# Retention and two mixture-of-experts layers in one kernel: the planned scheme of passes 1 and 2 used for pass 0 as well

## The chip, the cores and the metric

One core of one Trainium2 chip runs the whole program. The metric is device time in microseconds (us) for one execution, as the median of several; one further execution was recorded by the hardware profiler, and all rows below come from that one. The engines are PE (matrix products; PEld is its weight load), DVE, ACT and POOL (elementwise work), and SP, whose queue issues nearly all DMAs. Each engine works through its own instruction list in order.

## The reference, cut to what is computed

```python
# q, k, v: (4, 8, 576, 64); x: N = 2304 tokens of D = 512; E = 8 experts, F = 1024
ret = scale * (q @ k.T) * Dmat;  x = ret @ v          # retention
e = argmax(x @ w_gate)                                # layer 1: one expert for each token
x[mask_e] = gate * (relu(x[mask_e] @ w1[e]) @ w2[e])
P = exp(x @ w_gate2 - max); 8 times: rows and columns of P normalised   # layer 2
out = sum over e of P[:, e] * (relu(x @ w1[e]) @ w2[e])  # every token, every expert
```

Layer 2 is the bulk: all 2304 tokens go through all 8 experts. Each fp32 product is made of three products of a high and a low part (hi*hi, hi*lo, lo*hi), so each weight and each activation is split: ACT makes hi (a cast), DVE or POOL makes lo (value minus hi).

## The kernel before

Layer 2 runs in three passes of 768 tokens (`NP = 3`, `GRP = 384` columns for each half). In a pass an expert has four *units* (`i` = 0 to 3), each a quarter of its first product `x @ w1`. That product is done by a Strassen-Winograd scheme: 7 block products in place of 8 (`product(j)`, j = 0 to 6), each of 6 matmuls of 128x384, so 42 matmuls a unit. It needs sums of blocks of x (made once a pass, `xsums`, `xsplit`, `load_pass` in the changed kernel) and of w1 (made in pass 0 and stored, already split, in DRAM as `w1s`).

**Pass 0** (lines 1085 to 1292) is written out by hand. `unit()` takes the weights from a ring of slots (`Slot`, `split_step`, `keep_up`, lines 150 to 285): a kind of prefetch, in which two raw 256-column loads make two slots of kind "sums" (L255, L256 on POOL, L263 on ACT, L219 on DVE). The second product, `second()` (L1100 to L1102), is the plain one: 36 matmuls of 128x512 a unit, and it is always that of the unit before, set between the block products of the present one. So a unit has 42 + 36 matmuls, an expert 312. Into the first units other work is put with `mids`: the last second product of layer 1 (`last_steps`, 96 matmuls of 128x280, in unit 0), and the second gate with its 8 rounds of normalising (`sinkhorn`, `gate_step`). Until P is there, expert 0's result is kept unweighted, and `weigh` (L1124 to L1128) multiplies it afterwards.

**Passes 1 and 2** (lines 1299 to 1742) are made by a planner. Every instruction is a `Task` with an engine, an estimated duration and what it comes after; a list scheduler plays the tasks through, in order of due time, and issues the instructions of each engine in the order that results. The order on PE, `line`, is fixed ahead: the first product of expert s, with pieces of the second product of expert s-1 in its gaps (`GAPS`). The second product has 7 block products here too: `chunk2` (L1566 to L1568), 42 chunks of 6 matmuls of 128x256, 252 an expert, beside 168 of the first product (L1385 to L1387). For it, sums and splits are made of the hidden values (L1502, L1505, L1512, L219 on `sl`) and of w2 (L1502 and L1505 on POOL, L1512, L219 on `wbl`). Results go through `evict` (L1583, L1585) to `ya`. w1 is not made anew: `wa` is loaded from `w1s` (L1367).

Between the two lies a change of memory: `early.close()` gives the whole memory of pass 0 back, and the planner's tiles take it. `out` is written by indirect DMAs from POOL (L104).

```python
        GAPS = (1, 1, 2, 2, 1, 3, 0.5)
        for s in range(first_s, last_s + 1):
            b = [g2[s - 1, j, kh, t] for j in range(7) for kh in range(2) for t in range(HB)] if s > first_s else []
            ...
                    for j in range(7):
                        line.append(g1[s, i, j])
                        owed += GAPS[j]
                        while owed >= 1:
                            ...
                                line.append(b.pop(0))
```

Of the kernel before, what the change touches and what calls it, by code (L numbers as in the profile page):

```python
# [28 lines left out]
RAW = 5  # L29
LO_DVE = 256  # L30
LO_AT = 256
HI_DVE = ()
# [3 lines left out]
def kernel(  # L36
# [16 lines left out]
    dbg=None,  # L53
# [15 lines left out]
    raw_p = ctx.enter_context(tc.tile_pool(name="raw", bufs=RAW))  # L69

    early = ExitStack()
    ring_p = early.enter_context(tc.tile_pool(name="ring", bufs=4))
    sum_p = ctx.enter_context(tc.tile_pool(name="sums", bufs=1, side="right"))
# [66 lines left out]
    WEIGH_ACT = (0, 2, 4)  # L140
# [4 lines left out]
    WAIT = 4  # L145
    BEHIND = 6
    SPOTS = "bd"
# [6 lines left out]
    class Slot:  # L154
        def __init__(self, kind, parts, col=0):
            self.kind, self.parts, self.col = kind, parts, col
            slots.append(self)
            for r in parts:
                raws[r][3] = len(slots)
# [12 lines left out]
    def w1_slots(i):  # L172
        for f in range(2):
            Slot("plain", [part((i, f, r), lambda i, f, r: rows2(expert(w11, i), r)[:, :, f * half:(f + 1) * half])
                           for r in range(2)])

    def w2_slots(i):
        for f in range(2):
            Slot("plain", [part((i, f, r), lambda i, f, r: rows2(expert(w12, i), 2 * f + r))
# [26 lines left out]
    def load_more():  # L206
        while n_load[0] < n_known[0]:
# [5 lines left out]
            t = raws[n][2] = raw_p.tile([128, 1024], F32, tag="raw", name="raw")  # L213
# [7 lines left out]
    def split_step(n=1, force=False):  # L221
        for _ in range(n):
# [7 lines left out]
            need = c.parts[s // 2] if c.kind == "plain" else max(c.parts)  # L230
# [3 lines left out]
            if s == 0:  # L234
                c.hi = ring_p.tile([128, 2048], F32R, tag="hi", name="hi")
                c.lo = ring_p.tile([128, 2048], F32R, tag="lo", name="lo")
            if c.kind == "plain":
                x = raws[c.parts[s // 2]][2]
                o, i = s * 512, s % 2 * 512
                if s in HI_DVE:  # L240
# [1589 lines left out]
```

## Time and profile before

| | us |
|---|---|
| median of 3 runs (1873.04 to 1876.92) | 1876.38 |
| the profiled execution: time / span of its instructions | 1880.59 / 1878.8 |
| retention and layer 1, up to the first product of layer 2 | 0 to 377.8 |
| pass 0 | 377.8 to 890.8 |
| passes 1 and 2, to the last matmul | 890.8 to 1868 |

A page row of an engine gives its busy time, the share of the span and the count. A row of a stretch gives, for each engine, busy time and instruction count (x), then the granted share of TensorE's clock, the mean busy share of the DMA engines and GB/s. Since matmuls are pipelined, the count of matmuls in a stretch tells more than PE's busy time.

### The profile page before, as it was taken

Reading aid. Unit: us, or ns where it says so; the run is one execution under the profiler, and the core shown is the slowest. Engines: PE = TensorE matmul, PEld = TensorE weight load, DVE = VectorE, ACT = ScalarE, POOL = GpSimd, SP = SyncE. Lnnn points to the kernel's source line nnn. Section 1 sums busy time; section 2 is a strip of 40 time slices with the busy share of each in tenths; the row PEclk is TensorE's granted clock in tenths of the full one; section 3 lists DMA queues with packets and bytes.
Section 4 is the critical chain, followed back from the end, with each engine's and each line's share of the span. In section 5 each row is a group of like instructions: output and inputs, shape, how many; then the busy total and the mean of one; then the engine's idle time right before and its main releaser. Section 6 shows DMA issues by size and latency. Waiting matters only on the chain.

```text
span 1878.8 us, 32676 instructions
## 1 busy us (share of the span) xinstructions
PE 1803.9 (96%) x12227; PEld 1720.0 (92%) x12227; DVE 1233.2 (66%) x2239; ACT 892.2 (47%) x1718; POOL 575.1 (31%) x599
## 2 busy tenths in 40 slices
PE   7778999999999999999699999999999999999997
PEld 6657999998899999998599999999999999999997
DVE  6864446556655554555267777877887777777777
ACT  2243455544434343433355555555656555555553
POOL 4544567632332333334211121111223121111211
PEclk9998999999999999999899999999999999999998
DMA  9955555565555555543755555655556545555430
GB/s 261 239 162 176 174 196 185 175 217 184 185 186 185 185 185 204 199 174 121 229 167 152 165 160 169 186 162 153 162 165 197 155 154 161 167 158 166 145 123 35
DMA packets 194577, 325.13 MB, mean 173 GB/s; under 512 B 24547, under 2 KB 97507, under 8 KB 194408
## 3 DMA queue, kind: packets, MB, share of 16 engines
q1 hardware_dynamic: 190264, 312.29, 52.2%
q0 software_dynamic: 3712, 9.96, 1.7%
q8 instruction: 99, 1.62, 0.4%
q10 hardware_dynamic: 432, 0.69, 0.1%
q14 instruction: 70, 0.57, 0.1%
HBM read 248.28 MB, written 74.61 MB: 172 GB/s over the span
## 4 chain that ended last, share of the span: by engine, by line
PE 84%; DVE 3%; ACT 1%; issue 1%; DMA 1%; POOL 0%; SPq 0%; ACTq 0%; DVEq 0%; POOLq 0%
PE b L1568 8%; PE b L1567 8%; PE b L1566 8%; PE b L1385 8%; PE b L1386 8%; PE b L1387 8%; PE b L1100 5%; PE b L1102 5%; PE b L1101 5%; PE b L1170 4%; PE b L1172 4%; PE b L1171 4%; PE b L669 3%; PE b L671 3%; PE b L670 3%
## 5 line engine op out<-in xcount | busy, mean ns | idle before, releaser
L1566 PE MATMUL b<-wbh,sh 128*128 128x256 f32 x1344 | 379.7, 282 | 2.1 <-DVE ya L1585 2.1
L1568 PE MATMUL b<-wbh,sl 128*128 128x256 f32 x1344 | 380.3, 283 | 0.5 <-DVE sl L219 0.4
L1567 PE MATMUL b<-wbl,sh 128*128 128x256 f32 x1344 | 380.6, 283 | 0.0
L1385 PE MATMUL b<-ch,wa 128*128 128x384 f32 x896 | 304.8, 340 | 17.6 <-ACT kp L1391 7.4
L1386 PE MATMUL b<-cl,wa 128*128 128x384 f32 x896 | 302.3, 337 | 0.0
L1387 PE MATMUL b<-ch,wa 128*128 128x384 f32 x896 | 300.8, 336 | 0.0
L219 DVE TENSOR_TENSOR sl<-hq,sh 128x768 fp32r<-128x768 f32 x224 | 223.7, 1004 | 85.3 <-ACT sh L1512 83.2
L1568 PEld LDWEIGHTS b<-wbh,sl 128*128 128x128 f32 x1344 | 257.5, 192 | 0.9 <-DVE sl L219 0.9
L1566 PEld LDWEIGHTS b<-wbh,sh 128*128 128x128 f32 x1344 | 255.6, 190 | 2.3 <-ACT sh L1512 2.3
L1567 PEld LDWEIGHTS b<-wbl,sh 128*128 128x128 f32 x1344 | 257.2, 191 | 0.0
L219 POOL TENSOR_TENSOR lo<-raw,hi 128x256 fp32r<-128x256 f32 x192 | 171.8, 905 | 266.1 <-ACT hi L243 263.7
L1512 ACT CAST sh<-hq 128x768 fp32r<-128x768 f32 x224 | 184.5, 832 | 72.0 <-PE b L1567 67.3
L219 DVE TENSOR_TENSOR lo<-raw,hi 128x256 fp32r<-128x256 f32 (+1 forms) x256 | 152.2, 598 | 89.0 <-ACT hi L243 78.6
L1400 ACT ACTIVATE hq<-hq 128x384 f32<-128x384 f32 x192 | 100.9, 525 | 230.4 <-DVE hq L1397 228.4
L1385 PEld LDWEIGHTS b<-ch,wa 128*128 128x128 f32 x896 | 170.6, 190 | 22.7 <-ACT kp L1391 7.8
L1585 DVE SCALAR_TENSOR_TENSOR ya<-b,P,ya 128x256 f32<-128x256 f32 x312 | 142.2, 478 | 66.3 <-PE b L1568 65.0
L1502 POOL TENSOR_TENSOR raw<-raw 128x512 f32<-128x512 f32 x63 | 88.7, 1409 | 313.9 <-DVE wbl L219 219.6
L1386 PEld LDWEIGHTS b<-cl,wa 128*128 128x128 f32 x896 | 171.3, 191 | 0.0
L1387 PEld LDWEIGHTS b<-ch,wa 128*128 128x128 f32 x896 | 168.9, 189 | 0.0
L1170 PE MATMUL b<-ch,hi 128*128 128x384 f32 x448 | 151.6, 338 | 0.3
L1172 PE MATMUL b<-ch,lo 128*128 128x384 f32 x448 | 150.5, 336 | 0.0
L1171 PE MATMUL b<-cl,hi 128*128 128x384 f32 x448 | 150.3, 336 | 0.0
(212 smaller groups left out, 3729.8 us busy)
## 6 DMA issues: line engine op xcount, KB each, us to landing
wa<-w1s SPq DMA_DIRECT2D x192, 512.0 KB
raw<-in_moe_w_dram SPq DMA_DIRECT2D x128, 512.0 KB
w1s<-hi SPq DMA_DIRECT2D x32, 896.0 KB
w1s<-lo SPq DMA_DIRECT2D x32, 896.0 KB
raw<-in_moe_w_dram SPq DMA_DIRECT2D x108, 256.0 KB
wa<-w1s SPq DMA_DIRECT2D x64, 256.0 KB
sums<-in_moe_w_dram SPq DMA_DIRECT2D x20, 256.0 KB
kT<-in_kT_dram SPq DMA_DIRECT2D x18, 256.0 KB
```

The lines of the kernel that those rows point to most:

```text
L219: eng.tensor_tensor(lo, x, hi.bitcast(F32), ALU.subtract)
L1170: nc.tensor.matmul(ps, a, xh[:, r, :], start=first and r == 0, stop=False, skip_group_check=True)
L1171: nc.tensor.matmul(ps, a, xl[:, r, :], start=False, stop=False, skip_group_check=True)
L1172: nc.tensor.matmul(ps, b, xh[:, r, :], start=False, stop=r == 1, skip_group_check=True)
L1385: nc.tensor.matmul(ps, a, xh[:, r, :], start=first, stop=False, skip_group_check=True)
L1386: nc.tensor.matmul(ps, a, xl_[:, r, :], start=False, stop=False, skip_group_check=True)
L1387: nc.tensor.matmul(ps, b, xh[:, r, :], start=False, stop=r == 1, skip_group_check=True)
L1512: nc.scalar.copy(o.tile[0], src.tile)
L1566: nc.tensor.matmul(ps, hh[:, r, c], wh[:, r], start=st, stop=False, skip_group_check=True)
L1567: nc.tensor.matmul(ps, hh[:, r, c], wl[:, r], start=False, stop=False, skip_group_check=True)
L1568: nc.tensor.matmul(ps, hl[:, r, c], wh[:, r], start=False, stop=kh == 1 and r == 1, skip_group_check=True)
L1585: nc.vector.scalar_tensor_tensor(o, ps, sc_, o, ALU.mult, ALU.add)
```

## The change

- **Pass 0 joins the plan.** `unit`, `second`, `finish`, `weigh` and the slots for layer 2's weights are removed. The planner now runs over all 24 pairs of pass and expert (`n_exp = NP * E`).
- **w1 in pass 0** is made by tasks (`first_weights`): for each unit two loads of 128 columns (runs of 512 bytes; before, 256 columns for two units), four sums of 128x256 on POOL, a cast on ACT and a lo on DVE for each of four pieces (three of 512 columns, one of 256), and a store of each piece to `w1s`.
- **w2 in pass 0** and the second product go as in the later passes.
- **The last unit's second product of layer 1** is nine PE tasks (`tail`): four ahead of expert 0, the others between the first block products of its unit 0.
- **The second gate** is twelve PE tasks (`gate`), six between expert 0's products (`GATES`), six in expert 1's (`in_gap`); each is followed by a DVE task of 1.6 us that issues nothing and stands for what `gate_step` issued. Expert 0's results are weighted by six ACT tasks (`weighed`).
- **Expert 0** has no earlier second product to fill its gaps; its units are interleaved by hand instead (`line0`), with a second and third PSUM bank for it (`where`).
- **Memory** is given back in two lots: `early` when layer 1's last first product is issued (5 tiles `wa`, 9 `hq`, the raw tiles), `late` after `tail[8]` (`last_unit_done`: splits, `ya`, 4 more `hq`). The raw tiles and two ring tiles are fixed tiles of a pool `lot` that stays. `hq` has 13 tiles (before 14), `raw` 13 halves (before 12).
- **In all passes** the block products of the second product go in the order `JORD`, the pieces of w1 are grouped anew (`COLS`, `GROUP`), and the estimates are 0.722 us a chunk (before 0.714) and 1.3 us a POOL sum (before 1.45).

```diff
+    lot = ctx.enter_context(tc.tile_pool(name="lot", bufs=1))
+    rawt = [lot.tile([128, 1024], F32, name=f"raw{i}") for i in range(RAW)]
+    scr = lot.tile([128, 1024], F32, name="scr")
+    ringt = [None, None] + [lot.tile([128, 4096], F32R, name=f"ring{i}") for i in (2, 3)]
...
-    for p in range(1):
-        for e in range(E):
-            for j in range(2):
-                pr = [part((e, j, h), lambda e, j, h: w21[e][:, h * half + 256 * j:h * half + 256 * (j + 1)]
-                           .rearrange("(k p) f -> p k f", p=128)) for h in range(2)]
-                Slot("sums", pr, 0)
-                Slot("sums", pr, 128)
-                Slot("plain", [part((e, j, h), lambda e, j, h: rows2(w22[e], 2 * h + j)) for h in range(2)])
...
-        def second(u, rows_, half_f, tiles_, last):
-
...
-        def unit(u, pre, mids):
...
+    early.close()
+    new = fresh("early")
+    free = {
+        "w1": [two(x) for x in new("wa", 5, 1024, F32R)],
+        "h": [two(x) for x in new("hq", 9, 768)],
+        "raw": [two(x) for t in (*rawt, scr) for x in cut(t, [512] * 2)],
+        "s": [], "w2": [],
...
+    def last_unit_done():
+
+        pair = lambda a: tuple(two(x) for x in cut(a, [a.shape[1] // 2] * 2))
+        s0, s1, w0 = cut(ringt[2], [1536, 1536, 1024])
+        s2, w1_, w2_, w_hi = cut(ringt[3], [1536, 1024, 1024, 512])
+        late.close()
+        new = fresh("late", side="right")
+        free["s"] += [pair(x) for x in (s0, s1, s2)]
+        free["w2"] += [pair(x) for x in (w0, w1_, w2_)] + [(two(w_hi), two(w_lo))]
+        free["h"] += [two(x) for x in new("hr", 4, 768)]
+        acc.extend(new("ya", 3 * HB, 512))
+        free["raw"] += [two(x) for x in new("rw", 1, 512)]
...
+    GATES = {(0, 1): 4, (0, 5): 5, (1, 3): 6, (2, 1): 7, (2, 5): 4, (2, 3): 5}
+    in_gap = {}
+    JORD = (0, 1, 2, 5, 3, 4, 6)
+    W1_POOL = ()
+    COLS = {0: (0, 512), 1: (512, 1024), 2: (1024, 1536), 3: (1536, 1792)}
+    GROUP = {0: (0, 0), 1: (0, 256), 3: (1, 0), 4: (1, 256), 2: (2, 0), 6: (2, 256), 5: (3, 0)}
...
+    tail = []
+    for i in range(9):
+        tail.append(Task("PE", 1.56 if i < 8 else 0.01, lambda _: next(last, None), tail[-1:]))
+    gates = []
+
+    def gate(b):
+
+        g = Task("PE", 0.2, lambda _: gate_step(b), [tail[8], *gates[-1:]])
+        gates.append(Task("DVE", 1.6, None, [g]))
+        if len(gates) == 2:
+            there = Task("SP", 3.5, None, [g])
+            gates.append(Task("DVE", 0.3, lambda _: next(gate_queue[0]), [there]))
+        return g
+
...
+        fa, fb, sm = Buf("raw"), Buf("raw"), Buf("raw")
+        for d, b in enumerate((fa, fb)):
+            def load(_, b=b, d=d):
+                c = 512 * d + 128 * i
+                nc.sync.dma_start(out=b.tile.rearrange("p a (b f) -> p (a b) f", f=128),
+                                  in_=w21[e][:, c:c + 128].rearrange("(k p) f -> p k f", p=128))
+            b.load = Task("SP", 1.4, load, takes=b)
+        B = {(a, d): (lambda a=a, d=d: (fa, fb)[d].tile[:, a]) for a in range(2) for d in range(2)}
+        w5 = lambda: sm.tile[:, 0]
+        def split(gi, src, dep, uses):
+            c = COLS[gi][1] - COLS[gi][0]
+            o = wg[gi]
+            part_ = lambda k: o.tile[:, k, 0:c]
+            a = Task("ACT", c * 1e-3, lambda _: nc.scalar.copy(part_(0), src()), dep, takes=o, uses=uses)
+            pool = gi in W1_POOL
+            b = Task("POOL" if pool else "DVE", c * (2.6e-3 if pool else 1.17e-3),
+                     lambda eng: lo_of(eng, part_(1), src(), part_(0)), [a], uses=[o, *uses], wide=True)
+            def store(_, c0=COLS[gi][0]):
+                nc.sync.dma_start(out=w1s[n][:, :, c0:c0 + c], in_=f32(o.tile[:, :, 0:c]))
+            Task("SP", 4e-3 * c, store, [b], uses=[o])
+            o.load = b
+            return b
+        g0 = split(0, lambda: fa.tile.rearrange("p a f -> p (a f)"), [fa.load], [fa])
+        t5 = Task("POOL", 0.7, add(w5, B[0, 1], B[1, 1]), [fb.load], takes=sm, uses=[fb], wide=True)
+        t3 = Task("POOL", 0.7, sub(B[0, 1], B[0, 0], B[0, 1]), [t5, fa.load], uses=[fa, fb], wide=True)
+        t2 = Task("POOL", 0.7, sub(B[0, 0], w5, B[0, 0]), [t3, g0], uses=[fa, sm], wide=True)
+        t6 = Task("POOL", 0.7, sub(B[1, 0], B[1, 0], B[0, 0]), [t2], uses=[fa], wide=True)
+        split(1, lambda: fb.tile.rearrange("p a f -> p (a f)"), [t3], [fb])
+        split(2, lambda: fa.tile.rearrange("p a f -> p (a f)"), [t6], [fa])
+        split(3, w5, [t5, t2], [sm])
+        return wg
...
+            line0 = tail[0:4]
+            for n, j in enumerate((0, 1, 2, 5)):
+                line0 += [u[0][j], tail[4 + n]]
+            line0 += [u[0][3], tail[8]]
+            for i in range(4):
+                if i < 3:
+                    line0.append(u[i + 1][0])
+                line0 += [u[i][4], u[i][6]]
+                if i < 3:
+                    for j in (1, 2, 5, 3):
+                        line0.append(u[i + 1][j])
+                        if (i, j) in GATES:
+                            line0.append(gate(GATES[i, j]))
+            early_banks += gates
+        if e == E - 1 and p + 1 < NP:
+            last_of = dict(P_)
...
+                if s_ == 0:
+                    if fresh:
+                        nc.scalar.copy(o, ps)
+                    else:
+                        nc.vector.tensor_tensor(o, ps, o, ALU.add)
...
+
+            for i in range(3):
+                for j, bk in ((3, 1), (5, 0)):
+                    in_gap[i, j] = (gate(bk), gates[-1])
...
+                weighed[tt] = Task("ACT", 0.62, weigh, [gates[-1], *(ev[j, tt % HB] for j in jj)])
...
```

## Rows read from the trace of the kernel before

**Rows 1.** The page: busy us, share of span, instructions.
```profile
PE 1803.9 (96%) x12227; PEld 1720.0 (92%) x12227; DVE 1233.2 (66%) x2239; ACT 892.2 (47%) x1718; POOL 575.1 (31%) x599
```

**Rows 2.** Stretches of pass 0: busy us (count) by engine, clock, DMA, GB/s.
```profile
564.00:626.00 62.00, 62.00 (x314) 55.99 (x313) 32.77 (x59) 24.70 (x52) 19.27 (x24) 1.00 0.52 187
626.00:688.00 62.00, 62.00 (x313) 56.03 (x312) 32.49 (x59) 24.70 (x52) 19.27 (x24) 1.00 0.52 187
```

**Rows 3.** A stretch of pass 1, about one expert long.
```profile
1063.12:1122.18 59.06, 59.06 (x421) 59.06 (x421) 45.02 (x70) 31.47 (x57) 10.29 (x8) 1.00 0.52 160
```

**Rows 4.** PE's timeline: start, duration, instruction (pass 1; layer 1).
```profile
1068.93 0.28 PE L1566 MATMUL b<-wbh,sh 128*128 128x256 f32 x1
...
1070.37 0.34 PE L1385 MATMUL b<-ch,wa 128*128 128x384 f32 x1
...
1071.41 0.28 PE L1566 MATMUL b<-wbh,sh 128*128 128x256 f32 x1
...
364.15 0.29 PE L669 MATMUL b<-HH,hi 128*128 128x280 f32 x1
...
364.54 0.29 PE L669 MATMUL b<-HH,hi 128*128 128x280 f32 x1
```

**Rows 5.** Stretch: the first 59 us of the plan.
```profile
890.80:950.00 59.20, 42.74 (x215) 38.20 (x214) 16.55 (x25) 20.51 (x40) 13.14 (x13) 0.88 0.69 218
```

**Rows 6.** PE's timeline there; in brackets idle before, its end.
```profile
900.50 0.69 PE L1385 MATMUL b<-ch,wa 128*128 128x384 f32 x1 [7.44 <-ACT kp L1391]
...
942.23 0.44 PE L1385 MATMUL b<-ch,wa 128*128 128x384 f32 x1 [0.72 <-DVE hq L1397]
```

**Rows 7.** ACT's timeline, the same place.
```profile
899.97 0.48 ACT L1391 COPY kp<-b 128x384 f32<-128x384 f32 x1 [15.23 <-DMA out_dram<-a,idc]
```

**Rows 8.** Stretches around the start of pass 2.
```profile
1350.00:1390.00 40.00, 38.76 (x272) 38.15 (x272) 38.67 (x54) 22.92 (x40) 11.54 (x6) 1.00 0.44 135
1340.00:1400.00 60.00, 58.76 (x414) 58.15 (x413) 53.67 (x79) 36.39 (x63) 14.23 (x8) 1.00 0.50 157
```

**Rows 9.** DVE by shape, 950 to 1800: busy us, mean ns, idle.
```profile
L219 DVE TENSOR_TENSOR sl<-hq,sh 128x768 fp32r<-128x768 f32 x201 | 200.2, 1002 | 77.9 <-ACT sh L1512 75.8
L219 DVE TENSOR_TENSOR wbl<-raw,wbh 128x512 fp32r<-128x512 f32 x170 | 122.5, 722 | 1.5 <-ACT wbh L1512 1.5
L1502 DVE TENSOR_TENSOR hq<-hq,hq 128x768 f32<-128x768 f32 x88 | 86.2, 980 | 1.3
```

**Rows 10.** The same by tile: shortest/median/longest ns.
```profile
L219 DVE TENSOR_TENSOR sl<-hq,sh x201: 943/957/2050, 949.8 to 1798.0; 128x768 fp32r<-128x768 f32 x101
...
L219 DVE TENSOR_TENSOR wbl<-raw,wbh x170: 675/683/1791, 951.5 to 1799.3; 128x512 fp32r<-128x512 f32 x170
...
L1397 DVE TENSOR_TENSOR hq<-b,kp x57: 543/558/558, 961.6 to 1793.0; 128x384 f32<-128x384 f32 x57
```

**Rows 11.** Timeline of DVE and ACT, pass 0's start.
```profile
383.52 1.29 DVE L219 TENSOR_TENSOR lo<-sums,hi 128x512 fp32r<-128x512 f32 x2
...
370.80 0.40 DVE L219 TENSOR_TENSOR lo<-raw,hi 128x256 fp32r<-128x256 f32 x1
...
372.00 0.61 ACT L263 CAST hi<-raw 128x512 fp32r<-128x512 f32 x1
...
373.60 0.40 ACT L263 CAST hi<-raw 128x256 fp32r<-128x256 f32 x1
```

**Rows 12.** POOL by shape, 400 to 860: sums of w1.
```profile
L255 POOL TENSOR_TENSOR sums<-raw,sums 128x256 f32<-128x256 f32 x29 | 22.5, 778 | 0.0
```

**Rows 13.** SP's timeline at the second gate; stretches after it.
```profile
406.87 0.36 SPq L1016 DMA_DIRECT2D lg2d<-lgu  x1
408.15 0.41 SPq L1033 DMA_DIRECT2D lgall<-lg2d  x1
...
410.00:412.00 2.00, 2.00 (x12) 1.83 (x12) 1.22 (x3) 1.00 (x2) 0.00 (x0) 1.00 0.74 26
...
418.00:420.00 2.00, 2.00 (x13) 1.87 (x12) 0.89 (x2) 0.89 (x2) 0.00 (x0) 1.00 1.01 423
```

More of the change, by code (lines that the diff above doesn't have):

```diff
@@ L212, in load_more @@
             ap = make(*key)
[L213 removed]
+            t = raws[n][2] = rawt[n % RAW]
             raws[n].append(arrives(1.46))
@@ new lines @@
+    early.close()
[5 more added lines that the diff above has]
+        "s": [], "w2": [],
+    }
+    for k in ("p1", "u2", "u3"):
+        free[k] = new(k, 1, GRP)
+    w_lo, = new("wl", 1, 512, F32R)
+    acc = []
+    def last_unit_done():
[9 more added lines that the diff above has]
+        free["raw"] += [two(x) for x in new("rw", 1, 512)]
@@ new lines @@
+    line += b
+    clock_ = 0.0
+    for t in line:
+        t.ideal = clock_
+        clock_ += t.us
+    for t in tasks:
+        for a in t.after:
+            a.next.append(t)
+    order, left = [], {t: len(t.after) for t in tasks}
+    ready = [t for t in tasks if not left[t]]
+    while ready:
+        t = ready.pop()
+        order.append(t)
+        for n in t.next:
+            left[n] -= 1
+            if not left[n]:
+                ready.append(n)
+    assert len(order) == len(tasks)
@@ new lines @@
+    for t in reversed(order):
+        if t.eng == "PE":
+            t.due = t.ideal
+        for n in t.next:
+            t.due = min(t.due, n.due - t.us - LAG)
+    for t in tasks:
+        if t.takes:
+            takers.setdefault(t.takes.kind, []).append(t)
+    for k in takers:
+        takers[k].sort(key=lambda t: t.due)
+    import heapq
+    at = {k: 0.0 for k in ("PE", "ACT", "DVE", "POOL", "SP")}
+    eng_of = {"ACT": nc.scalar, "DVE": nc.vector, "POOL": nc.gpsimd, "PE": nc.tensor, "SP": nc.sync}
@@ new lines, with free_of, start @@
+    waits = {t: len(t.after) for t in tasks}
+    able = {k: [] for k in at}
+    pool_until = [0.0]
+    n_pe, pipe, t_now = [0], [0.0], 0.0
+    num = {t: n for n, t in enumerate(tasks)}
+    for t in tasks:
+        if not waits[t] and t.eng != "PE":
+            able[t.eng].append(t)
+    ends = []
+    busy = {}
+    def free_of(kind):
+        while busy.get(kind) and busy[kind][0][0] <= t_now:
+            free[kind].append(heapq.heappop(busy[kind])[2])
+        return free[kind]
+    def start(t):
+        us = t.us
+        if t.takes:
+            t.takes.tile = free[t.takes.kind].pop(0)
+            takers[t.takes.kind].pop(0)
+            t.takes.left = len(t.takes.users)
+        if t.fn:
+            t.fn(eng_of[t.eng])
+        if t.eng == "SP":
+            pipe[0] = max(pipe[0], t_now) + us
+            t.end = pipe[0] + 2.5
+            at["SP"] = t_now + 0.1
+        else:
+            if t.eng == "DVE" and t.wide and pool_until[0] > t_now:
+                us *= 1.4
+            if t.eng == "POOL" and t.wide:
+                pool_until[0] = t_now + us
+            at[t.eng] = t_now + us
+            t.end = t_now + us + LAG
+        heapq.heappush(ends, (t.end, num[t], t))
```

1002 lines of the change are left out of this document (384 added, 618 removed).

## The prediction

> **What bounds the kernel now.** I read the page's busy times first: PE is busy 96% of the span, DVE 66% [rows 1]. So PE sets the time, and only two things can bring any back: fewer or shorter matmuls, and stretches in which PE waits. The views by stretch show both. Inside pass 0 a stretch of 62.00 us holds 313 or 314 matmuls, with PE busy throughout and DVE for about 32.5 us [rows 2]; an expert of 312 matmuls takes 62.0 x 312 / 313.5 = 61.7 us. Inside pass 1, 59.06 us hold 421 shorter matmuls, again without a gap, and DVE works 45.0 us [rows 3]; an expert of 420 takes 58.9 us. The timeline agrees: two chunks of the second product take 1.44 us, a block product of the first 1.04 [rows 4], and 28 x 1.04 + 42 x 0.72 = 59.4. The one long stretch in which PE waits is the first 59 us of the plan: 215 matmuls [rows 5], by the cadences 168 x 0.173 + 47 x 0.120 = 34.7 us of work, so 24.5 us lost. PE first waits 7.4 us for ACT, which waits for a scatter of the old accumulator, since `kp` lies in its memory [rows 6, 7]; then, with nothing between the block products, 0.57 to 0.72 us at each of a dozen evictions [rows 6]; and the granted clock over the stretch is 0.88 [rows 5], so that part of it ran on the lower level, 1.2 GHz.
>
> **The change part by part.** The sum is made against the profiled execution, 1880.6 us.
>
> *Second product of pass 0 by the scheme.* PE does 252 matmuls of 256 columns in place of 144 of 512: 61.7 - 58.9 = 2.8 us an expert, 8 experts, **-22 us**.
>
> *The break between pass 0 and 1 goes.* The 24.5 us at 890.8 go with the change of memory. What is late next is what is late at the start of pass 2, where the plan also changes its x: 40 us there hold 38.76 us of PE [rows 8], 1.3 us lost. Net **-23 us**.
>
> *Last unit's product and gate matmuls.* They remain. Pass 0 took 513 us; 8 x 61.7 is 494, the 96 matmuls of the last unit at 0.13 [rows 4] are 12.5, and some 7 us are left for gate matmuls and short waits. I give back 3 of these: between none and all 7. **-3 us**.
>
> *A new cold start.* Expert 0 has no second product to fill its gaps, as expert 8 had none at 890.8. For it speaks that nine pieces of the last unit (12.5 us) and interleaved units lie between a product and the one that needs its eviction: one block product or more, 1.04 us [rows 4], against the wait of 0.57 to 0.72 when they were adjacent [rows 6]. So an eviction is hidden if ACT is free, and costs some tenths behind a cast of 0.61 us [rows 11]. I take 4 us for 28 products. The gate adds: from the store of its logits to the end of the slow stretch that follows its load (26 GB/s at a DMA share of 0.74) lie over 5 us [rows 13], and before the store a transpose, a reduction and SP. The plan gives this 3.5 + 2.5 us, the path is nearer to 9; the product line holds 8 products, 8.3 us, before the next gate, but the DVE instruction that waits for the load sits in DVE's queue where the plan put it, with the adders of expert 0 behind it and PE behind those: 3 us. Three later gates stand only one to four products apart, each with a chain of some eight small DVE operations: 3 us. The loads need no room: the DMA engines moved 423 GB/s when asked [rows 13], and expert 0's 11 MB fit well into 41 us. In all **+10 us**; 3 if the cover holds, 24.5 if it is as cold as the old start was.
>
> *DVE in pass 0.* This is the price. To the 45.0 us of a later-pass expert [rows 3] come the lo parts of w1: 12 of 512 columns at 0.61 (two take 1.29 together) and 4 of 256, about 0.31 each [rows 11], 8.5 us. And POOL gets 16 sums of 0.78 us [rows 12] more, 22.7 us in place of 10.3. Those lengthen DVE: operations with both inputs in SBUF have means above their medians (1002 against 957 ns, 722 against 683) [rows 9, 10], over 14 + 14 + 8 of them 1.4 us an expert, 0.13 us for each us of POOL; the adder that reads PSUM runs from 543 to 558 and is never lengthened [rows 10]. With the two-input share of DVE up by 39.1 / 30.6, 22.7 x 0.13 x 1.28 = 3.8 us, 2.4 more than now. So DVE has 45.0 + 8.5 + 2.4 = 56 of 58.9 us to do: 95%. The trace has one stretch like that, the renewing of x before pass 2: DVE 38.67 of 40 us busy, PE short by 1.24, or 3.1% [rows 8]. I take 3.1% of 7 x 58.9 us: **+13 us**; the least is 0, since PE has 58.9 us of its own, the most is rival 3. ACT rises from 31.5 us [rows 3] by 12 x 0.61 + 4 x 0.40 [rows 11] to 40 of 59, and waits for no one longer.
>
> *Queues.* SP's queue is in order: each of 16 stores of w1 an expert waits for a lo of DVE, and loads behind it wait too. They are for buffers 30 us ahead (13 raw halves, 22 uses an expert), so a DVE late by a few us costs nothing; if that cover is gone, it adds the same lateness, not more. Weighting by ACT instead of ACT and POOL, one hidden tile less and the order `JORD` I cost at nothing: PE has no gap in passes 1 and 2 [rows 3], and the last two block products that end the kernel keep their places relative to the scatters. Layer 1 no longer shares its last units with w1's splits; PE was full there.
>
> Sum: -22 - 23 - 3 + 10 + 13 = -25, so 1855 for an execution like the profiled one. That one lay 4.2 us above the median of the runs; taken off, **1851 us**.
>
> **The rivals.**
> 1. *The covers are complete*: cold start 4, DVE 2. Then -48 + 6 = -42, 1834 us. For it: PE shows no gap at DVE shares up to 45 of 59 us [rows 3], and splits can be made ahead. Against: rows 8.
> 2. *The start is as cold as before*, 24.5 us, as gate and chains meet: -48 + 24.5 + 13, 1866 us. For it: the same 28 products without fill lost that [rows 5, 6]. Against: 7.4 of it was the scatter, much of the rest the low clock that followed.
> 3. *Slower: POOL shuts DVE out.* In pass 0 DVE's two-input operations (39 us) and POOL's sums (22.7 us) together want more than an expert's 58.9 us. If they exclude each other, DVE becomes the bound. Without lengthening DVE has 52.2 us; the gains left, 48 - 10 = 38 us over 7 experts, are 5.5 each, so this decides from 64.4 us, that is when 12.2 of POOL's 22.7 us are lost to DVE, 54%. The longest rows do show that: a split of 957 ns took 2050 and one of 683 took 1791 [rows 10], 1.1 us beside a sum of about 1.3. If DVE lost POOL's time in proportion to its own two-input share, 39.1 / 58.9 of 22.7 = 15.1 us, an expert would take 67.3: 7 x 8.4 = 59, so -48 + 10 + 59 = +21, 1897 us. Against: the mean loss was 0.13 us for a us of POOL [rows 3, 9, 10]. The Trainium skill (SBUF — State Buffer, "Who interferes with whom") says that a DVE instruction with two SBUF inputs contends with a GpSimd one that reads SBUF, and calls the shared ports an exclusive lock. By that rule the 1897 us would hold; the trace agrees that only two-input operations are lengthened (PSUM adder 558 at most), not that each meeting costs all of it.
> 4. *DVE sustains less than the 97% of those 40 us.* Over the best 60 us it was busy 53.67, 89.5% [rows 8]; 56 / 0.895 = 62.6 us an expert, +26 in place of +13: 1864 us.
>
> **How the numbers follow.** Forecast 0.50, own range 1842 to 1862; rival 1 0.17; rival 2 0.14; rival 4 0.06; rival 3 0.08; 0.05 for something between 3 and the others that ends within 0.2%, about 3.8 us, which is what a measurement of this kernel can tell from no change. Faster by more: 0.87; the same 0.05; slower 0.08. Half of rival 1 and all of rival 3 and that between are left outside: 1833 to 1873.
>
> **What would show it.** Each expert of pass 0 from the second on: 420 matmuls in 59 to 61 us (right), 62 or more (rival 4), 65 or more (rival 3), and DVE busy some 55 us of each 59. Splits of 512 columns with a mean near 0.78 us; above 1.0 is rival 3. No wait of over 2 us between pass 0 and 1 and a granted clock of 1.00 there. In expert 0, idle PE of 10 us in all, the longest wait at the gate's load; with 20 us and a clock under 1.00 it is rival 2. The forecast is wrong if PE waits for weights in expert 0 (`wa` late from DMA or POOL), which I costed at nothing, or if passes 1 and 2 no longer run without gaps.

## The result, and the profile after

The changed kernel took 1895.82 us (median of 10 runs, 1889.37 to 1901.43), the kernel before 1878.06 (10 runs, 1873.04 to 1887.08) in the same sessions: a ratio of 1.0093, interval 1.0073 to 1.0112. It is slower by 0.9%; the forecast was 1851 us, and the range ended at 1873. The profiled execution took 1895.59 us.

The page's busy times after, to be held against [rows 1]:

```profile
PE 1792.8 (95%) x13091; PEld 1753.7 (93%) x13091; DVE 1465.8 (77%) x2456; ACT 1010.8 (53%) x1887; POOL 664.6 (35%) x589
```

Two stretches of the new pass 0 and one of pass 1, each one expert long (columns as in [rows 2, 3]):

```profile
537.84:596.76 58.92, 55.72 (x386) 54.62 (x385) 53.23 (x77) 34.91 (x66) 26.80 (x22) 1.00 0.57 191
596.76:655.68 58.92, 56.16 (x387) 55.55 (x386) 54.83 (x78) 36.60 (x67) 26.62 (x22) 0.97 0.53 179
1068.12:1127.04 58.92, 58.92 (x421) 58.92 (x420) 46.13 (x69) 31.55 (x57) 12.57 (x8) 1.00 0.54 161
```

Pass 1 is as before: 421 matmuls in an expert's time. In pass 0 only 386 or 387 fit into the same time, and DVE is busy for 53 to 55 us of it. The clock is full or nearly so: PE waits.

From the timeline of PE I took, for each expert, the time from its first block product to that of the next. Before, an expert of passes 1 and 2 took 59.2 us by this measure, and the first planned one (expert 8, at the break) 52.6 us, where its own 168 matmuls are 29. After, in us:

| | before | after |
|---|---|---|
| expert 0 + expert 1 (full PE: 29.1 + 6.2 for four tail pieces + 59.2 = 94.5) | | 49.2 + 78.1 = 127.3 |
| experts 2 to 7 | 61.7 each [rows 2] | 63.9, 64.2, 64.1, 65.1, 64.2, 67.7 |
| expert 8, the change to pass 1 | 52.6, without a second product beside it | 61.6 |
| experts of passes 1 and 2 | 59.2 | 59.2 |
| change to pass 2 | 61.2 | 61.2 |

So the time was lost in two places, both ahead of expert 9: 32.8 us over the first two experts and 34.0 us over the next six (389.2 - 6 x 59.2). From expert 9 on both kernels keep the same pace; expert 9 starts at 960.4 us after and at 943.4 us before, and the 17 us between them are the result but for 2. Of the 17, 4.4 lie ahead of the first block product of layer 2 (377.9 us before, 382.3 after), which now stands behind four tail pieces.

What PE waited for in most of pass 0 (440 to 860 us: sum, times, longest):

```profile
PE b L1292 <- ACT u L1298: 12.0, 14, 1.9
PE b L1450 <- DVE ring L211: 6.9, 8, 2.0
PE b L1448 <- ACT ring L1394: 6.3, 1, 6.3
PE b L1292 <- DVE hr L1304: 3.5, 4, 1.3
```

The first row names ACT, which is not short of time (35 of 59 us). One of the 14 waits, in the timelines of PE, ACT, DVE and POOL (start, duration, instruction, idle before):

```profile
584.49 0.44 PE L1292 MATMUL b<-ch,wa 128*128 128x384 f32 x1 [1.85 <-ACT u L1298]
```

```profile
579.39 0.46 ACT L1298 COPY u<-b 128x384 f32<-128x384 f32 x1
582.19 0.62 ACT L1242 CAST wa<-raw 128x512 fp32r<-128x512 f32 x1 [2.34 <-POOL raw L1142]
582.72 0.82 ACT L1394 CAST ring<-hq 128x768 fp32r<-128x768 f32 x1
583.45 0.61 ACT L1394 CAST ring<-raw 128x512 fp32r<-128x512 f32 x1
583.97 0.47 ACT L1298 COPY u<-b 128x384 f32<-128x384 f32 x1
```

```profile
575.68 0.82 DVE L211 TENSOR_TENSOR wa<-raw,wa 128x512 fp32r<-128x512 f32 x1
576.42 2.04 DVE L211 TENSOR_TENSOR ring<-hq,ring 128x768 fp32r<-128x768 f32 x1
578.38 0.55 DVE L1304 TENSOR_TENSOR hq<-b,p 128x384 f32<-128x384 f32 x1
578.85 0.76 DVE L211 TENSOR_TENSOR wl<-raw,ring 128x512 fp32r<-128x512 f32 x1
579.53 2.03 DVE L1145 TENSOR_TENSOR hr<-hq,hq 128x768 f32<-128x768 f32 x1
```

```profile
575.91 1.74 POOL L1142 TENSOR_TENSOR raw<-scr,raw 128x512 f32<-128x512 f32 x1
577.60 3.14 POOL L1142 TENSOR_TENSOR raw<-raw,raw 128x256 f32<-128x256 f32 x2
580.70 1.46 POOL L1142 TENSOR_TENSOR raw<-raw 128x256 f32<-128x256 f32 x1
582.12 1.98 POOL L1145 TENSOR_TENSOR raw<-raw,raw 128x512 f32<-128x512 f32 x1
```

Read from PE backwards: it waits for the copy `u` of 583.97; that stands in ACT's queue behind a cast of w1 which sat idle for 2.34 us until a sum of POOL was ready; that sum was one of a row in which a pair of 128x256 took 3.14 us (0.78 each was the mean before, [rows 12]). On DVE, at the same time, splits and sums of 768 columns take 2.03 and 2.04 us (median before 957 ns, [rows 10]), while the adder that reads PSUM takes its 0.55. So three readings were open: DVE has too much to do by itself; POOL and DVE lengthen each other (one operation takes longer because the other engine works at the same time); or nobody is short, and the plan put ACT's queue into a bad order, with casts ahead of `u` that wait for POOL.

### The profile page after: what moved, and what is told of

Read it like the earlier page. It is cut to its first block, busy times and chain, and to the rows that moved or that the text cites. A ratio compares the mean times of both kernels' runs of the same rounds, so it can differ in the third digit from the quotient of the medians.

```text
span 1893.8 us, 35494 instructions
## 1 busy us (share of the span) xinstructions
PE 1792.8 (95%) x13091; PEld 1753.7 (93%) x13091; DVE 1465.8 (77%) x2456; ACT 1010.8 (53%) x1887; POOL 664.6 (35%) x589
## 4 chain that ended last, share of the span: by engine, by line
PE 67%; DVE 11%; issue 6%; POOL 4%; DMA 1%; ACT 1%; SPq 0%; POOLq 0%; DVEq 0%; ACTq 0%
PE b L1450 11%; PE b L1449 10%; PE b L1448 10%; PE b L1292 10%; PE b L1293 10%; PE b L1294 10%; DVE ring L211 3%; POOL ring L211 2%; PE b L641 2%; DVE ya L1477 1%; DVE hq L1142 1%; PE b L643 1%; PE b L642 1%; DVE wa L211 1%; DVE hq L1304 1%
## 5 line engine op out<-in xcount | busy, mean ns | idle before, releaser
L1450 PE MATMUL b<-ring,ring 128*128 128x256 f32 x1176 | 333.3, 283 | 4.3 <-DVE ring L211 4.3
L1448 PE MATMUL b<-ring,ring 128*128 128x256 f32 x1176 | 332.6, 283 | 0.0
L211 DVE TENSOR_TENSOR ring<-hq,ring 128x768 fp32r<-128x768 f32 x239 | 251.0, 1056 | 70.6 <-ACT ring L1394 70.2
L1292 PE MATMUL b<-c,wa 128*128 128x384 f32 x896 | 301.9, 337 | 1.0 <-DVE hq L1304 0.5
L1293 PE MATMUL b<-c,wa 128*128 128x384 f32 x896 | 301.0, 336 | 0.0
L1294 PE MATMUL b<-c,wa 128*128 128x384 f32 x896 | 299.4, 334 | 0.0
L211 DVE TENSOR_TENSOR ring<-raw,ring 128x512 fp32r<-128x512 f32 (+1 forms) x312 | 233.9, 751 | 64.8 <-ACT ring L230 50.7
L1448 PE MATMUL b<-ring 128*128 128x256 f32 x840 | 238.1, 283 | 8.5 <-ACT ring L1394 6.3
L1450 PE MATMUL b<-ring 128*128 128x256 f32 x840 | 238.5, 284 | 4.7 <-DVE ring L211 4.7
L1449 PE MATMUL b<-ring,ring 128*128 128x256 f32 x840 | 238.3, 284 | 0.0
L1450 PEld LDWEIGHTS b<-ring,ring 128*128 128x128 f32 x1176 | 225.6, 192 | 5.4 <-DVE ring L211 5.4
L1394 ACT CAST ring<-hq 128x768 fp32r<-128x768 f32 x239 | 197.3, 833 | 59.4 <-PE b L1449 47.3
L1448 PEld LDWEIGHTS b<-ring,ring 128*128 128x128 f32 x1176 | 223.8, 190 | 0.1
L1449 PE MATMUL b<-ring 128*128 128x256 f32 x672 | 190.7, 284 | 0.0
L1394 ACT CAST ring<-raw 128x512 fp32r<-128x512 f32 x261 | 160.8, 617 | 45.8 <-PE b L1450 43.2
L1292 PE MATMUL b<-ch,wa 128*128 128x384 f32 x448 | 157.5, 352 | 24.9 <-ACT u L1298 12.0
L1292 PEld LDWEIGHTS b<-c,wa 128*128 128x128 f32 x896 | 169.7, 189 | 1.8 <-DVE hq L1304 1.1
L1293 PEld LDWEIGHTS b<-c,wa 128*128 128x128 f32 x896 | 170.2, 190 | 0.0
```

The lines of the kernel that those rows point to most:

```text
L211: eng.tensor_tensor(lo, x, hi.bitcast(F32), ALU.subtract)
L1292: nc.tensor.matmul(ps, a, xh[:, r, :], start=first, stop=False, skip_group_check=True)
L1293: nc.tensor.matmul(ps, a, xl_[:, r, :], start=False, stop=False, skip_group_check=True)
L1294: nc.tensor.matmul(ps, b, xh[:, r, :], start=False, stop=r == 1, skip_group_check=True)
L1394: nc.scalar.copy(o.tile[0], src.tile)
L1448: nc.tensor.matmul(ps, hh[:, r, c], wh[:, r], start=st, stop=False, skip_group_check=True)
```

## The experiments

The theory: POOL's sums lengthen DVE's two-input operations (those with both inputs in SBUF), and this alone takes pass 0 past its cadence, the 59.2 us that PE needs for an expert. The rivals: DVE's own load (rival 4 of the prediction); the order of the plan, or its tiles; the chain from POOL's sums to the casts. Retention and layer 1 are the same in the kernels made from the changed one, and yet the first block product of layer 2 starts ("first start") anywhere from 374.8 to 386.2 us in their profiled executions. Each row of the table is one execution. So I compare what lies behind that start: the first two experts together, and the mean of experts 2 to 6. The last two columns are from the stretch 510 to 830 us. How well the pace repeats is seen where an edit alters nothing behind expert 1: e4 has 64.3 like the changed kernel, h3 59.3 like f2.

| kernel | total | first start | experts 0 + 1 | experts 2 to 6, mean | DVE busy of 320 | POOL busy |
|---|---|---|---|---|---|---|
| after | 1895.6 | 382.3 | 127.3 | 64.3 | 299.9 | 144.2 |
| e1, no w1 sums | 1877.1 | 382.4 | 126.8 | 61.8 | 300.0 | 71.4 |
| e2, half of w1's lo on ACT | 1878.6 | 378.4 | 126.3 | 62.7 | 289.0 | 146.2 |
| e3, six wa | 1913.5 | 384.7 | 128.5 | 67.2 | 287.7 | 158.3 |
| e4, one round | 1877.7 | 374.8 | 118.0 | 64.3 | 299.4 | 143.4 |
| f1, e1 and e2 | 1863.6 | 381.3 | 124.0 | 60.2 | 289.4 | 68.2 |
| f2, no sums on POOL | 1857.1 | 385.8 | 120.4 | 59.3 | 282.1 | 0 |
| g1, true durations | 1901.6 | 385.9 | 123.2 | 64.5 | 302.8 | 152.4 |
| h1, sums for nobody | 1896.9 | 375.9 | 130.1 | 64.7 | 304.6 | 150.5 |
| h2, w2's sums on DVE | 1884.0 | 386.2 | 126.3 | 62.6 | 305.8 | 86.8 |
| h3, f2 and one round | 1841.1 | 376.9 | 113.6 | 59.3 | 281.0 | 0 |

**e1: no w1 sums on POOL.**

```diff
-        t5 = Task("POOL", 0.7, add(w5, B[0, 1], B[1, 1]), ...
+        t5 = Task("POOL", 0.7, None, ...        # t3, t2, t6 the same; w5 is a part of fb
```

> The changed kernel without the four sums of w1 blocks that POOL makes for each unit of pass 0 (the products use unsummed blocks; the plan keeps the tasks' places and durations). Theory: from expert 2 on pass 0 is bound by DVE, which has about 60 us of work for each 64.1 us expert, some 9 us of it lengthening by POOL; 16 of 24 POOL operations go, so DVE falls to about 54.5 us and an expert takes 59 to 60.5 us, the run 25 to 35 us less than the changed kernel (1860 to 1870). Rival 1 (the tiles wa, held until their stores to DRAM are done, or SP's in-order queue, set the pace): an expert stays at 63 to 64.5 us, the run within 5 us. Rival 2 (DVE is the bound by its own work, POOL's share is small): 62 to 63 us, the run 8 to 12 us less.

Measured: 61.8 us an expert, between the two expectations of the theory and of rival 2. DVE stayed as busy as it was, 300 of 320 us, and did more experts in that time: 57.9 us of work each, not the 54.5 expected. The eight sums of 128x512 that stayed lengthened DVE by 6.7 us an expert (34.8 us in 320, below), where the theory left them some 2.

**e2: half of w1's low parts by ACT.**

```diff
-                     lambda eng: lo_of(eng, part_(1), src(), part_(0)), ...
+                     half_lo, ...    # columns from c // 2 on: nc.scalar.copy(lo, x)
```

> The changed kernel in which half of each lo part of w1 in pass 0 is made by ACT as a plain cast (its values are wrong), so that DVE has 4.3 us less for each expert and ACT some 5 us more; POOL's sums stay. Theory (DVE bound): an expert of pass 0 takes 60 to 61 us in place of 64.1, the run 18 to 26 us less. Rival 1 (wa tiles, stores, SP's order): 63 to 64.5 us, the run within 5 us of the changed kernel.

Measured: 62.7, which neither side expected. DVE's work went from 60.3 to 56.6 us an expert (busy share times the expert's time), and only 1.6 us came back. With DVE busy for 90% PE still waits: the share of DVE isn't the whole story.

**e3: a sixth wa tile in place of one raw half.**

```diff
-        "w1": [two(x) for x in new("wa", 5, 1024, F32R)],
+        "w1": [two(x) for x in new("wa", 6, 1024, F32R)],
...
-        free["raw"] += [two(x) for x in new("rw", 1, 512)]
```

> The changed kernel with six tiles wa in place of five and twelve raw halves in place of thirteen; the result is unchanged. Theory (DVE bound): an expert of pass 0 stays at 63.5 to 64.5 us, the run within 5 us. Rival 1 (five wa tiles, each held until its store is done, set the pace): 60 to 62 us, the run 12 to 25 us less.

Measured: 67.2 us, 3 us worse, outside both expectations. More room for w1 at the price of a raw half didn't help; the plan's order changed, and POOL was busier. What a sixth `wa` alone would do was not run. But in the changed kernel PE waited for w1 only once from 440 to 860 us, for 0.6 us (`DVE wa`).

**g1: the plan is given the durations of the trace** (w1's lo parts, evictions, adders, gate steps and the reload of the logits too).

```diff
-        t5 = Task("POOL", 0.7, ...          t3 = Task("POOL", 1.3, ...
+        t5 = Task("POOL", 1.05, ...         t3 = Task("POOL", 1.7, ...
-    UB, US = (0.51, 0.60), (0.73, 0.87)
+    UB, US = (0.51, 0.68), (0.73, 0.95)
```

> The changed kernel with nothing but the plan's durations altered to those that the trace showed (POOL sums 0.7 to 1.05 and 1.3 to 1.7 us, VectorE splits and sums up by 0.08, evictions by 0.06, gate steps 1.6 to 2.2, the reload of the logits 3.5 to 7 us); every instruction stays, their order changes. If the wrong order on ScalarE (the copy of u behind a cast that waits for a POOL sum) is the loss, the experts of the first pass fall from 64.1 to 61 or below and the start by some 5 us: total 1865 to 1878. If the load itself is the bound, the order gives under 1 us per expert: 63 to 65 us an expert and a total of 1885 to 1900.

Measured: 64.5 us an expert and 1901.6 in all. What PE waits for (440 to 860 us) is another thing now:

```profile
PE b L1448 <- ACT ring L1394: 10.2, 7, 1.5
PE b L1450 <- DVE ring L211: 8.4, 7, 2.9
PE b L1292 <- DVE hq L1304: 4.8, 5, 1.7
PE b L1292 <- DVE hr L1304: 4.8, 3, 3.3
```

The waits for `u` are down to 0.4 us in all, and the time is the same. The row "ACT u" of the changed kernel named the place where the shortage showed, not its cause: with the wait for `u` gone nothing is won, so that order of ACT's queue was not the loss. That no other order would do better is not shown.

**f1 and f2: both reliefs; no sum on POOL at all.**

```diff
+            # f2, beside e1:  t3, t5, t2, t4 of w2 in the first pass
-            t3 = Task("POOL", 1.3, sub(T3[kh], B[1, 1], B[0, 1]), ...
+            t3 = Task("POOL", 1.3, sub(T3[kh], B[1, 1], B[0, 1]) if p else None, ...
```

> The changed kernel without the 16 POOL sums per expert of the first pass's first weights, and with half of each of those weights' low parts made by a plain ScalarE copy instead of VectorE's three-input operation (both leave out part of the computation). Each of the two alone brought the experts of the first pass from 64.1 to about 62 us. If the loss is VectorE's load plus its lengthening beside POOL, the two add: 64.1 less 2.2 less 1.5 is 60.4 us an expert, floor 58.9 to 59.2, and VectorE idles over 12% of 510 to 830 us. If something else holds the pass at 62 (ScalarE's order, the chain through the sums of the second operand), taking both away leaves 61.5 to 62.5 us.

> The changed kernel without any POOL sum in the first pass, neither of the first nor of the second weights (part of the computation is left out; all splits, loads and stores stay). VectorE's work is whole, its contention gone. If contention is what stretched VectorE past the cadence, its 56 us per expert fit again: 59 to 60.3 us an expert, total 20 to 30 us below the changed kernel, that is 1866 to 1876. If VectorE's own load at 95% cannot be scheduled without loss (my fourth rival), it stays at 61.5 to 62.5 us as with only the first weights' sums removed, total about 1876.

Measured: f1 60.2, f2 59.3 us an expert, both as the theory had it; f1's DVE idled for 10% and not for 12, and f2's total of 1857.1 lies under its range, since the first two experts gained 6.9 us too. The stretch 510 to 830 us of f2, and its splits and sums by tile (shortest/median/longest ns), to be held against the same view of the changed kernel, which stands behind it:

```profile
510.00:830.00 320.00, 320.00 (x2269) 319.61 (x2268) 282.12 (x462) 214.75 (x389) 0.00 (x0) 1.00 0.61 197
```

```profile
L211 DVE TENSOR_TENSOR ring<-hq,ring x51: 948/955/960, 518.3 to 824.1; 128x768 fp32r<-128x768 f32 x51
L211 DVE TENSOR_TENSOR ring<-raw,ring x46: 679/684/692, 509.8 to 827.9; 128x512 fp32r<-128x512 f32 x46
```

```profile
L211 DVE TENSOR_TENSOR ring<-hq,ring x47: 943/959/2050, 525.4 to 811.0; 128x768 fp32r<-128x768 f32 x47
L211 DVE TENSOR_TENSOR ring<-raw,ring x39: 674/684/1785, 513.6 to 827.5; 128x512 fp32r<-128x512 f32 x39
```

In f2 PE has no gap in 320 us, with DVE busy for 88% of them, and not one split is lengthened: 948 to 960 ns, all 51. In the changed kernel the median is the same and the longest is twice as long. DVE's own work is 282.12 x 59.3 / 320 = 52.3 us an expert, and that fits: DVE's own load costs nothing. Rival 4, a limit of 89.5% on DVE, isn't tested by f2's 88%; it falls by the changed kernel itself, whose DVE was busy for 94% of 320 us, and by h2 below with 96%.

**h1: the sums again, but for nobody.**

```diff
-        t5 = Task("POOL", 0.7, None, ...
+        t5 = Task("POOL", 0.7, idle_sum(...), ...     # junk <- B[0, 1] - B[1, 1]; all 24 an expert
```

> The kernel of f2_no_pool_at_all, in whose first pass POOL now makes all 24 sums of an expert again, of the same shapes, from the same loaded buffers, but into a scratch tile that nobody reads (part of the computation is still left out). So POOL's work is back and no one waits for a result of it. If POOL's sums cost by lengthening VectorE's operations, the loss comes back: 62.5 to 64.5 us an expert from the third on, VectorE busy 297 us or more of 510 to 830, and a total of 1880 to 1896. If they cost because the casts wait for their results, it stays at 59.3 to 60.5 us and 1857 to 1865.

Measured: 64.7 us an expert, 1896.9 in all, both just above the range: the changed kernel's time, and that with a first start 6.4 us earlier. No cast and no split waits for these sums, and from 440 to 860 us SP's queue, which loads the buffers that they read, never waited for POOL either; the sums only run. That the loss comes back in full, with 51.6 us of lengthening on DVE (below), shows that it is the lengthening, and not the chain from the sums to the casts.

```profile
510.00:830.00 320.00, 304.03 (x2079) 298.95 (x2078) 304.58 (x423) 193.89 (x357) 150.48 (x115) 0.98 0.56 184
```

**h2: w2's sums of the first pass on DVE.**

```diff
-            t3 = Task("POOL", 1.3, ...
+            t3 = Task(*(("POOL", 1.3) if p else ("DVE", 0.68)), ...      # t5, t2, t4 the same
```

> The changed kernel with the 8 sums of 128x512 per expert of the second weights made by VectorE instead of POOL in the first pass; the 16 sums of the first weights stay on POOL. VectorE gets 8 x 0.68 = 5.5 us of its own work. From the runs with and without these sums they lengthen VectorE by some 6 us when POOL makes them. If that is so, VectorE is as busy as before (298 to 302 of 320 us), no result comes late, and an expert takes 62 to 64 us, total 1882 to 1895: POOL's help is worth nothing there. If POOL's lengthening is less than VectorE's own work, VectorE becomes the bound: 65 us or more and a total over 1898.

Measured: 62.6 us an expert. DVE was given 8 sums more, 5.5 us an expert by their median of 0.68, and pass 0 went faster by 1.7 us an expert. (DVE was busier than expected, 305.8 of 320 us against 298 to 302.) For these sums POOL's help is worth less than nothing.

*The price of a meeting.* With f2's lengths as base (954, 683 and 418 ns) I added up, from DVE's timeline of 510 to 830 us, what each operation with two SBUF inputs took above its base (of the kernel before in pass 1, 960 to 1280 us). The lengthenings are not spread: most operations have none, and the rest gather at about 1.1 us where the sums have 512 columns (a good part of them at 0.6 and below), and at 0.55 or 0.4 where they have 256.

| kernel | sums on POOL | added to DVE, us | for each sum |
|---|---|---|---|
| before, pass 1 | 44 of 128x512 | 9.2 | 0.21 |
| e1 | 45 of 128x512 | 34.8 | 0.77 |
| h2 | 82 of 128x256 | 20.4 | 0.25 |
| after | 40 of 128x512, 80 of 128x256 | 45.6 | |
| h1 | 37 of 128x512, 78 of 128x256 | 51.6 | |

Two neighbours in e1, on DVE and on POOL, show one such meeting; alone the first takes 0.95 us and the second 1.3:

```profile
640.23 1.94 DVE L1142 TENSOR_TENSOR hr<-hq,hr 128x768 f32<-128x768 f32 x1
```

```profile
639.46 1.89 POOL L1142 TENSOR_TENSOR raw<-raw,raw 128x512 f32<-128x512 f32 x1
```

A meeting costs up to 1.1 us for 512 columns and up to 0.55 for 256, whichever DVE operation it is. A sum that starts inside such an operation gets longer itself (1.75 us on average in e1, against 1.30 for the others). In pass 1 of the kernel before a sum cost a fifth of that on average, in e1 70%. DVE has a two-input operation under way more often there (39 against 31 of 59 us, without lengthening), but that alone is not a factor of four. The rest is when the sums start. In pass 1 only 3 of the 44 began while a two-input operation was under way, and 30 began while DVE was idle: many of them had waited for a split of DVE to end, and DVE then paused. Such a start, on POOL and on DVE:

```profile
1057.20 1.29 POOL L1505 TENSOR_TENSOR raw<-raw 128x512 f32<-128x512 f32 x1 [1.79 <-DVE wbl L219]
```

```profile
1056.37 0.68 DVE L219 TENSOR_TENSOR wbl<-raw,wbh 128x512 fp32r<-128x512 f32 x1
1058.21 0.56 DVE L1397 TENSOR_TENSOR hq<-b,kv 128x384 f32<-128x384 f32 x1 [1.16 <-PE b L1387]
```

In e1, where DVE hardly pauses, 31 of 44 began inside a two-input operation. A sum overlapped with such operations for 0.33 us on average in pass 1 and for 1.36 us in e1, much the same factor of four (the lengthening itself is counted in the overlap). The Trainium skill (SBUF — State Buffer, "Who interferes with whom") calls the shared ports an exclusive lock; the trace agrees, at a price for each meeting that the sum's width sets.

**e4 and h3: the start.**

```diff
         for it in range(8):
-            nc.vector.tensor_reduce(rs, P, AX.X, ALU.add)
+            if it == 0: ...            # the five operations ahead of the gate's matmul
             nc.tensor.matmul(o[:, 0:E], ones, ce, start=True, stop=True)
+            if it: continue            # the three behind it
```

> The changed kernel with only the first of the eight rounds of normalising P; the other rounds keep their matmul on PE and their place in the plan but issue nothing on DVE (7 rounds of about 2.1 us). Theory for the start (experts 0 and 1 took 49.2 and 78.1 us, some 32 us more than their matmuls need): DVE is the bound there too and the rounds are 15 us of its work, so expert 1 falls to 62 to 68 us and the run is 10 to 16 us less. Rival (the start is lost to the gate's DRAM round trip on SP's queue and to memory that comes late): expert 1 stays at 74 or more, the run within 5 us.

> The kernel of f2_no_pool_at_all with one round of normalising instead of eight on VectorE (both leave out part of the computation; the gate's matmuls stay). The first two experts took 127.3 us in the changed kernel, 120.4 without POOL's sums, 117.9 with one round; 94.6 would be full PE from the start of the first. If the two causes are separate, both away give 110 to 113 us, and 15 to 18 us of loss are left for the load of the logits and the missing second product. If they overlap, 116 or more.

Measured: the first two experts take 127.3 us as changed, 118.0 with one round, 120.4 without POOL's sums, 113.6 without either. Of the 17.9 us by which e4's total is lower, 9.4 are this and 7.5 are an earlier first start. Expert 1 took 73.2 us in it, which neither the theory (62 to 68) nor the rival (74 or more) had, and h3's 113.6 lies just above the range for separate causes. Of the 32.8 us lost, the rounds hold 7 to 9 and POOL 4 to 7; 19.1 are left with both gone. In the changed kernel two stretches show it:

```profile
410.00:430.00 20.00, 11.65 (x55) 10.46 (x55) 13.74 (x37) 7.46 (x16) 5.23 (x7) 0.91 1.00 315
460.00:470.00 10.00, 2.72 (x9) 2.43 (x10) 9.76 (x20) 3.80 (x7) 1.09 (x3) 0.57 0.26 79
```

At 410 to 430 the DMA engines are full and DVE is not. PE waits 1.9 us at 411 for `m`, the maximum of the reloaded logits, and 3.1 us at 420 for a cast of w1 whose load SP could issue only at 408.8 us, behind the reload. At 460 to 470 DVE has no pause and PE gets nine matmuls: I read this as the debt of DVE, rounds and lengthened splits together; f2, without the sums, still has 23 matmuls and DVE at 7.9 of 10 us there. Of the 19 us in h3 the waits that the trace names are 8.3; in h3 the granted clock lay at 0.80 to 0.85 from 400 to 430 us, so part of that time ran on the lower level, 1.2 GHz. I didn't take it apart further.

**c1 and c2: the break of the kernel before, mended by itself.** If the changed memory was what brought the break's 24.5 us, a smaller edit of the kernel before should bring them too. c1 lays the tiles `kp`, `ku`, `kv` out ahead of `hq`, so that they don't lie on the accumulator that is being scattered. c2 also interleaves the units of expert 8, as the change does for expert 0, with banks 2 and 3 for them.

```diff
         free = {
             "w1": slots_of("wa", 5, (128, 2, 512), F32R),
             ...
+            "p1": slots_of("kp", 1, (128, GRP)),
+            "u2": slots_of("ku", 1, (128, GRP)),
+            "u3": slots_of("kv", 1, (128, GRP)),
             "h": slots_of("hq", 14, (128, 2, GRP)),
...
+            if s == first_s:                                          # c2
+                line += [u[0][j] for j in (0, 1, 2, 5, 3)]
+                for i in range(4):
+                    if i < 3: line.append(u[i + 1][0])
+                    line += [u[i][4], u[i][6]]
+                    if i < 3: line += [u[i + 1][j] for j in (1, 2, 5, 3)]
```

> The kernel before, its three keeper tiles kp, ku and kv laid out ahead of the hq tiles, so that kp no longer lies on the memory of an accumulator that is still being scattered at the break between the first two passes; nothing else is altered. If the break's loss of 24.5 us began with that wait of 7.4 us and the lower clock that followed the idle TensorE, the break shrinks to 8 to 17 us of loss and the total falls by 7 to 16 us, to 1860 to 1870. If other waits of the break (the new operand's sums, the first weights) end at nearly the same time, under 4 us are gained: 1872 or more.

> The kernel of c1_keepers_first with the units of the first planned expert also interleaved, as the changed kernel does for its first one: next unit's first product ahead of this unit's last two, and banks 2 and 3 for them. c1 gained 8 us of the break's 24.5. PE still waited some 10 us in it between the block products for ScalarE's copies and VectorE's adders, and the clock was lower. If the interleaving hides these, another 6 to 10 us: 1862 to 1867. If the first weights' loads or the operands of the second product end the waits instead, under 3 us more: 1869 to 1873.

Measured, each against the kernel before in the same session: c1 1872.27 us against 1880.58, ratio 0.9955 (0.9932 to 0.9977). c2 **1860.05 us against 1876.46, ratio 0.9919 (0.9893 to 0.9945)**. Expert 8 takes 52.6 us before, 45.4 in c1 and 37.2 in c2, where 29 would be full PE; pass 0 ahead of it takes 513 us in all three. PE's waits from 870 to 960 us in c1 and in c2:

```profile
PE b L1385 <- ACT ku L1391: 5.1, 4, 2.0
PE b L1385 <- DVE hq L1397: 2.9, 4, 0.7
PE b L1385 <- ACT kv L1391: 2.3, 4, 0.6
```

```profile
PE b L1389 <- DMA wa<-w1s: 4.8, 3, 2.5
PE b L1389 <- ACT kv L1395: 0.6, 1, 0.6
```

The scatter's 7.4 us [rows 6, 7] are gone in c1, the waits for evictions in c2, and what ends late then is the load of the first weights. By the two ratios c2 lies 1.7% under the changed kernel (0.9919 / 1.0093); the two were not run side by side.

## Why the prediction was wrong

In the forecast's own terms, counted from the first block product to expert 9: full PE would take 94.5 + 7 x 59.2 = 508.9 us, the changed kernel took 578.1, so 69 us were lost. The forecast had 28.

| loss | forecast | measured |
|---|---|---|
| experts 0 and 1: cold start 10, DVE 1.9, gate matmuls and short waits 4 | 16 | 32.8 |
| experts 2 to 7: DVE | 11 | 34.0 |
| expert 8: the new pass | 1.3 | 2.4 |

- **The second product by the scheme, -22: right as a gain of PE, and not collected.** With POOL silent an expert of pass 0 takes 59.3 us (f2) against 61.7: 2.4 us, 19 over eight. As changed it takes 64.3.
- **The break, -23: right.** Expert 8 now loses 2.4 us. c1 and c2 show that the reasons were the ones read from [rows 6, 7]: first the scatter, then the evictions with nothing between.
- **The covers at nothing: right but for one.** Passes 1 and 2 run without a gap, and a sixth wa tile in place of a raw half (e3) doesn't help. But PE waited 3.1 us for w1 in expert 0, behind SP's queue, its longest wait there; the forecast had named this as a thing that would make it wrong. After that it was 0.6 us.
- **DVE's own work in pass 0: right.** 45.0 + 8.5 less the 1.4 us of lengthening gave 52.1; f2 shows 52.3.
- **The lengthening by POOL: this is the step that failed.** I took 0.13 us for each us of POOL from pass 1 and scaled it by DVE's share to 3.8 us an expert. It is 9.2 (45.6 us in 320, at 64.3 an expert). The mean of pass 1 was no rate: it was a price of up to 1.1 us for each meeting, few of which happened there, because the sums began in DVE's pauses (13 of 196 two-input operations were lengthened by over 0.3 us, in the changed kernel 67 of 260). A pass 0 with DVE nearly full leaves them no pauses. The longest rows of [rows 10], 2050 and 1791 ns, showed the price, and I set them aside for the mean. POOL's own time was mis-sized in the same way, 22.7 us forecast against 29.0 (144.2 x 64.3 / 320), since the sums are lengthened too.
- **DVE's shortage, +13: mis-sized as a result.** Own work and lengthening together were 60.3 us of DVE an expert by its busy time (299.9 of 320 us), more than the cadence of 59.2: DVE could not keep up, and no loss of 3.1% beside a PE that is still the bound could stand for it. The other 4 us up to 64.3 are DVE's pauses, 20 of 320 us. That sum isn't all of it: DVE's work was under the cadence in e1 (57.9) and e2 (56.6), and still 2.6 and 3.5 us an expert were lost. A single lengthened operation also comes late for whoever waits for it; how the loss divides between the two the runs don't say.
- **The cold start, +10: too low by 17.** The 10 us of idle PE expected in expert 0 came (8.9 of 49.3 us, clock 0.96); the larger loss, 18.9 of the 32.8 us, fell in expert 1. The forecast took no account of POOL, which costs 4 to 7 over the two, nor of what the eight rounds take from DVE (7 to 9); I had charged only the chains of three later gates, 3 us. The 19 us that h3 leaves are close to the 16 forecast.
- **The rivals.** Rival 3 named the mechanism and a time of 1897, at a chance of 0.08; it decides from 64.4 us an expert, and the six experts took 64.9 on average. Its own size was too high, 15.1 us of lengthening and 67.3 an expert; that its total of 1897 fits is luck, since the start was worse than it had it. Rival 2's sign, 20 us of idle PE in expert 0, did not come, though its size did: 33 us of loss over two experts, with a clock of 0.57 in one stretch of expert 1. Rival 4 came near in pace (62.6 us an expert) for the wrong reason: DVE does sustain 94% (300 of 320 us). Rival 1's DVE at no more than 2 us is what f2 shows, without POOL.

The signs that the prediction named were the right ones, and they pointed between: splits of 512 columns with a mean of 0.73 to 0.91 us (478 to 832 us; columns as in [rows 9]), where 0.78 was forecast and 1.0 was rival 3.

```profile
L211 DVE TENSOR_TENSOR ring<-raw,ring 128x512 fp32r<-128x512 f32 x46 | 41.8, 908 | 0.0
L211 DVE TENSOR_TENSOR wa<-raw,wa 128x512 fp32r<-128x512 f32 x48 | 34.8, 726 | 1.5 <-ACT wa L1242 1.5
```

## What to carry to other kernels

Where two engines lengthen each other, take the price from the longest rows and the number of meetings from how full both will be and when their operations will start: a mean from a stretch in which one of them has pauses says little about one in which it has none. A sum given to POOL beside a DVE that is nearly full can be dearer than the same sum on DVE (h2); what PE is seen to wait for there (ACT's copies) can be moved about by the order without a gain (g1). And where a change is one gain that stands in the trace and one that has a price, make the first alone: c2 takes 15 us of the break with one order, two banks more and three tiles moved.

## What the runs showed of the hardware that I had not expected

A DVE operation with two SBUF inputs that meets a POOL sum is lengthened by up to 1.1 us for a sum of 128x512 and up to 0.55 for 128x256, whatever its own length; over half of such operations in the changed kernel show nothing of it. Retention and layer 1, the same instructions in the changed kernel and the ten made from it, ended anywhere within 11 us (first block product of layer 2 at 374.8 to 386.2 us), nearly as much as h2 gained in all (1895.6 to 1884.0).
